# A fused attention and mixer kernel: the order and the queues of its opening loads

## The chip, the cores and the metric

The kernel runs on one core of a Trainium2 chip. The metric is the device time of one execution in microseconds (us); lower is better.

## The reference

Everything starts from one layer norm of x (2048 tokens of 512 values). One branch is attention with 32 heads of 128 against a cached K and V; the other is a mixer with an MLP, whose result gates the attention.

```python
xn = _layernorm(x, axis=-1)
s = _A_ref(xn, A_k_cache, A_v_cache, A_wq, A_wo)     # q = xn @ wq; softmax(q k^T) v; @ wo
g = _silu(_B_ref(xn, B_w1, B_w2, B_w3, B_w4))        # h = gelu(layernorm(xn) @ w1); shifts; @ w2; MLP
return x + s * g
```

## The kernel before

**The whole.** The tokens are cut into 16 tiles of 128. The opening normalises them, transposes them into `xnT` and runs the mixer (`m1`, `m2`) and the first query projections (`q_ahead`). The MLP follows (`m3`, `m4`). Then a long loop over 128 units (8 groups of 4 heads, 4 blocks of 512 tokens) does scores, exponentials, the product with V and the output projection. All but the opening is untouched here.

**What sets the order.** Each engine runs its instructions in the order in which the program writes them: `pin` is the scheduler's `keep_in_program_order`. A DMA is an instruction of the engine that issues it. So what stands behind a waiting DMA issue on ScalarE's queue waits as well, and so on SP's (`nc.sync`).

**The opening loads (L466 to L476).** `load_x` (L159) loads one token tile of 128 KB, `load_w` (L153) the query weights of one head, 128 KB, on SP unless told otherwise. `w1_sb` is the mixer weight, loaded as two halves of 256 KB; `w2_sb` is 512 KB. The line with `junk` (L472) is an activation of one column; ahead of it stands the fetch of the GELU table into ScalarE. In this text x0 is token tile 0, wq0 the query weights of head 0, and so on. The two queues hold before the change:

- ScalarE: x1, x3, the second half of w1, wq0, wq1, wq2, then the table fetch and the small activation
- SP: x0, x2, the first half of w1, x4, x5, x6, x7, wq3, w2, and (L534) x8 to x15

**What uses them.** `ln1(t)` (L489) runs on VectorE: the statistics of tile t+1 (`bn_stats`, L180), then the norm of tile t (L185), with a power on GpSimd in between (L175, L176). `tr_pe(t)` (L195) transposes a tile with four matmuls on TensorE, and ScalarE copies it out of PSUM (L199) into `xnT`. All matmuls go through the helper at L109, so the trace knows them by their tiles: `ps_o<-ident,xall` is a transpose, `ps_m<-xnT,w_sb` the mixer's first product for one tile (`m1_tile`, L495), `ps_q<-xnT,wq_h` a query projection. TensorE's order from L511 on is: transposes of tiles 0 and 1, m1 of tile 0, transposes of tile 2, m1 of tile 1, transposes of tile 3, m1 of tiles 2 and 3; then, four times, a query projection (heads 0 to 3) and the transposes of one of the tiles 4 to 7; then `m2`, which needs w2. Tiles 8 to 15 are transposed by DMA, issued from SP (`tr_dma`, L201), and behind these SP issues the query weights of the last four heads (`wq_e`, L551) and w3. A projection with `wq_e` follows the third block of m1.

Of the kernel before, what the change touches and what calls it, by code (L numbers as in the profile page):

```python
# [17 lines left out]
def kernel(  # L18
# [15 lines left out]
    nc = tc.nc  # L34
# [16 lines left out]
    HG = 4  # L51
# [10 lines left out]
    pin = tc.keep_in_program_order  # L62
# [41 lines left out]
    w1_v = B_w1.rearrange("(dc p) j -> p dc j", p=P)  # L104
# [3 lines left out]
    def mm(out, lhsT, rhs, start, stop):  # L108
# [9 lines left out]
        out=ident[:], in0=diag[:], scalar1=0.0, scalar2=None, op0=ALU.is_equal))  # L118
# [34 lines left out]
    def load_w(h, eng=nc.sync):  # L153
        wqs[h] = wqp.tile([P, DC, Dh], BF16, name="wq_h")
        pin(eng.dma_start(out=wqs[h][:], in_=wq_v[:, :, h * Dh:(h + 1) * Dh]))
# [3 lines left out]
    def load_x(t, eng):  # L159
        xin[t] = tokp.tile([P, D], BF16, tag="ta", bufs=10, name="xin")  # L160
        pin(eng.dma_start(out=xin[t][:], in_=xsrc[t]))
# [3 lines left out]
    w1_sb = pL.tile([P, DC, D], BF16, name="w1_sb")  # L165
# [297 lines left out]

    for t, eng in enumerate([nc.sync, nc.scalar, nc.sync, nc.scalar]):  # L466
        load_x(t, eng)
    pin(nc.sync.dma_start(out=w1_sb[:, 0:2, :], in_=w1_v[:, 0:2, :]))
    pin(nc.scalar.dma_start(out=w1_sb[:, 2:4, :], in_=w1_v[:, 2:4, :]))
    for h in range(HG - 1):  # L470
        load_w(h, nc.scalar)
    pin(nc.scalar.activation(out=junk[:], in_=ones_t[:], func=ACT.Gelu_apprx_tanh))  # L472
    for t in range(4, 8):
        load_x(t, nc.sync)
    load_w(HG - 1)
    pin(nc.sync.dma_start(out=w2_sb[:], in_=w2_v))  # L476
    wps = psX.tile([P, 512], FP32, tag="xm", name="ps_warm")

# [139 lines left out]
    for g in range(NG - 1):  # L618
        b = (g * QT + QT - 1) * HG
        for hh in range(HG):  # L620
            h = (g + 1) * HG + hh
# [234 lines left out]
```

## Time and profile before

| | us |
|---|---|
| median of 3 runs | 1258.79 |
| range of the runs | 1258.17 to 1259.65 |
| the profiled execution | 1256.22 |
| its span, first to last instruction | 1254.4 |

The span is the time from the first to the last instruction of the profiled execution; the rest of its time lies around it. Instructions have their engine, the line of the kernel, the operation, the tile written and the tile read; times run from the span's start. An engine name with q (SPq, ACTq) is its sequencer issuing a DMA. "Busy" is the time an engine worked, and a wait is put down to what came last by the profile.

### The profile page before, as it was taken

Reading aid. Unit: us, or ns where it says so; the run is one execution under the profiler, and the core shown is the slowest. Engines: PE = TensorE matmul, PEld = TensorE weight load, DVE = VectorE, ACT = ScalarE, POOL = GpSimd, SP = SyncE. Lnnn points to the kernel's source line nnn. Section 1 sums busy time; section 2 is a strip of 40 time slices with the busy share of each in tenths; the row PEclk is TensorE's granted clock in tenths of the full one; section 3 lists DMA queues with packets and bytes.
Section 4 is the critical chain, followed back from the end, with each engine's and each line's share of the span. In section 5 each row is a group of like instructions: output and inputs, shape, how many; then the busy total and the mean of one; then the engine's idle time right before and its main releaser. Section 6 shows DMA issues by size and latency. Waiting matters only on the chain.

```text
span 1254.4 us, 16268 instructions
## 1 busy us (share of the span) xinstructions
PE 1237.3 (99%) x5814; PEld 598.7 (48%) x5931; DVE 1031.8 (82%) x1430; ACT 1100.4 (88%) x1117; POOL 35.3 (3%) x91
## 2 busy tenths in 40 slices
PE   8999999999999999999999999999999999999998
PEld 4444444444444444444444444444444444444443
DVE  7721567788988988898888988888888999978888
ACT  4444888999999999999999999999999999998886
POOL 4320000000000000000000000000000000000000
PEclk9999999999999999999999999999999999999999
DMA  6492011435234533544244423453244534442222
GB/s 168 106 163 68 15 28 43 85 85 97 59 78 104 106 52 76 97 102 85 59 90 98 105 48 85 88 118 68 55 102 97 105 68 84 97 93 53 68 56 59
DMA packets 224945, 103.86 MB, mean 83 GB/s; under 512 B 176928, under 2 KB 208160, under 8 KB 224864
## 3 DMA queue, kind: packets, MB, share of 16 engines
q1 hardware_dynamic: 221904, 99.93, 38.0%
q0 software_dynamic: 672, 1.84, 0.9%
q10 hardware_dynamic: 2288, 1.05, 0.3%
q8 instruction: 46, 0.75, 0.3%
q14 instruction: 35, 0.29, 0.1%
HBM read 67.90 MB, written 2.36 MB: 56 GB/s over the span
## 4 chain that ended last, share of the span: by engine, by line
PE 96%; DVE 2%; DMA 1%; issue 1%; ACT 1%; SPq 0%; DVEq 0%; ACTq 0%
PE ps_s L109 39%; PE ps_o L109 36%; PE ps_q L109 9%; PE ps_wo L109 9%; PE ps_m L109 2%; DMA w_sb<-in_B_w_dram 0%; DVE acc L302 0%; DMA rb<-dr 0%; PE ps_sum L109 0%; PE ps_w L109 0%; DMA wq_h<-in_A_wq_dram 0%; ACT qT L277 0%; DVE y L392 0%; DVE xall L420 0%; ACT pT L291 0%
## 5 line engine op out<-in xcount | busy, mean ns | idle before, releaser
L291 ACT ACTIVATE pT<-ps_s 128x1024 bf16<-128x1024 f32 x1024 | 1034.5, 1023 | 76.1 <-PE ps_s L109 28.3
L109 PE MATMUL ps_s<-qT,kT 128*128 128x512 bf16 x2041 | 607.5, 379 | 0.6
L109 PE MATMUL ps_o<-pT,vb 128*128 128x512 bf16 x1962 | 589.0, 379 | 0.5
L302 DVE TENSOR_TENSOR acc<-acc,pT 128x2048 bf16<-128x2048 bf16 x255 | 309.1, 1212 | 77.3 <-ACT pT L291 72.7
L109 PEld LDWEIGHTS <-kT 128*128 128x128 bf16 x2048 | 231.2, 113 | 226.1 <-issue 0.8
L109 PEld LDWEIGHTS <-vb 128*128 128x128 bf16 x2048 | 200.3, 98 | 225.9 <-issue 0.3
L109 PE MATMUL ps_wo<-wo_h,oT 128*128 128x512 bf16 x492 | 177.8, 379 | 2.1
L109 PE MATMUL ps_q<-xnT,wq_h 128*128 128x512 bf16 x481 | 172.9, 379 | 2.1
L297 DVE TENSOR_TENSOR acc<-pT 128x2048 bf16<-128x2048 bf16 x128 | 155.7, 1216 | 6.0 <-ACT pT L291 5.9
L358 DVE TENSOR_TENSOR oT<-ps_o,rb 128x512 bf16<-128x512 f32 x127 | 124.4, 980 | 23.1 <-DMA rb<-dr 22.7
L307 DVE TENSOR_TENSOR acc<-acc 128x1024 bf16<-128x1024 bf16 x127 | 87.8, 692 | 4.3
L275 DVE CAST qT<-ps_q 128x512 bf16<-128x512 f32 x112 | 76.4, 682 | 0.3 <-PE ps_q L109 0.3
L109 PEld LDWEIGHTS <-oT 128*128 128x128 bf16 x508 | 48.5, 98 | 56.2 <-DVE oT L358 0.7
L109 PEld LDWEIGHTS <-wq_h 128*128 128x128 bf16 x484 | 47.2, 98 | 56.1 <-issue 0.2
L411 DVE TENSOR_TENSOR sacc<-ps_wo,sacc 128x512 f32<-128x512 f32 x96 | 66.3, 690 | 3.2 <-PE ps_wo L109 2.7
L338 DVE TENSOR_REDUCE sm<-tT 128x4 f32<-128x512 bf16 x96 | 65.3, 681 | 0.0
L308 DVE TENSOR_TENSOR acc<-acc 128x512 bf16<-128x512 bf16 x127 | 54.0, 425 | 4.3
L242 ACT ACTIVATE h2T<-ps_s 128x1024 bf16<-128x1024 f32 x28 | 28.6, 1023 | 24.1 <-PE ps_s L109 24.1
L109 PE MATMUL ps_s<-xn2T,w_sb 128*128 128x512 bf16 x219 | 48.6, 379 | 0.3
L109 PEld LDWEIGHTS <-w_sb 128*128 128x128 bf16 x336 | 30.4, 98 | 34.5 <-issue 2.3
L109 PEld LDWEIGHTS <-h2T 128*128 128x128 bf16 x224 | 21.5, 98 | 25.0 <-issue 0.2
L109 PE MATMUL ps_m<-w_sb,h2T 128*128 128x512 bf16 x106 | 31.0, 379 | 0.5
(75 smaller groups left out, 333.4 us busy)
## 6 DMA issues: line engine op xcount, KB each, us to landing
rb<-dr SPq DMA_DIRECT2D x127, 256.0 KB, 4.0
vb<-in_A_v_cache_dram SPq DMA_DIRECT2D x64, 256.0 KB, 3.1
wo_h<-in_A_wo_dram SPq DMA_DIRECT2D x32, 128.0 KB, 3.0
wq_h<-in_A_wq_dram SPq DMA_DIRECT2D x29, 128.0 KB, 3.3
w_sb<-in_B_w_dram SPq DMA_DIRECT2D x8, 256.0 KB, 5.7
kT<-in_A_k_cache_dram SPq DMA_TRANSPOSE x128, 3.1
xl<-in_A_x_dram SPq DMA_DIRECT2D x16, 128.0 KB, 3.8
dr<-rc SPq DMA_DIRECT2D x127, 2.0 KB, 1.4
```

Source lines behind the costliest of these rows:

```text
L109: pin(nc.tensor.matmul(out=out, lhsT=lhsT, rhs=rhs, start=start, stop=stop))
L242: pin(nc.scalar.activation(out=h2[c, f][:], in_=ps[:], func=ACT.Gelu_apprx_tanh))
L275: pin(nc.vector.tensor_copy(out=qT[:], in_=st[u].pop("psq")[:]))
L291: pin(nc.scalar.activation(out=s["pT"][-1][:, jj:jj + 2, :], in_=sps[:], func=ACT.Exp, scale=SCALE))
L297: pin(nc.vector.tensor_tensor(out=s["acc"][:], in0=s["pT"][0][:], in1=s["pT"][1][:], op=ALU.add))
L302: pin(nc.vector.tensor_tensor(out=a[:], in0=a[:], in1=st[u]["pT"][i][:], op=ALU.add))
L307: pin(nc.vector.tensor_tensor(out=a[:, 0:2, :], in0=a[:, 0:2, :], in1=a[:, 2:4, :], op=ALU.add))
L308: pin(nc.vector.tensor_tensor(out=a[:, 0, :], in0=a[:, 0, :], in1=a[:, 1, :], op=ALU.add))
L338: pin(nc.vector.tensor_reduce(out=sm[:], in_=s["tT"][:], axis=mybir.AxisListType.X, op=ALU.add))
L358: pin(nc.vector.tensor_tensor(out=to, in0=o, in1=rb, op=ALU.mult))
L411: pin(nc.vector.tensor_tensor(out=sa, in0=ps[:], in1=sa, op=ALU.add))
```

## The change

ScalarE's queue is made to hold x1, the second half of w1, x3, and then the table fetch. All four query weights go to SP's queue, behind x4 to x7 and ahead of w2. Nothing else differs; the loads are the same in number and size.

```diff
-    for t, eng in enumerate([nc.sync, nc.scalar, nc.sync, nc.scalar]):
+    for t, eng in enumerate([nc.sync, nc.scalar, nc.sync]):
         load_x(t, eng)
+    pin(nc.scalar.dma_start(out=w1_sb[:, 2:4, :], in_=w1_v[:, 2:4, :]))
     pin(nc.sync.dma_start(out=w1_sb[:, 0:2, :], in_=w1_v[:, 0:2, :]))
-    pin(nc.scalar.dma_start(out=w1_sb[:, 2:4, :], in_=w1_v[:, 2:4, :]))
-    for h in range(HG - 1):
-        load_w(h, nc.scalar)
+    load_x(3, nc.scalar)
     pin(nc.scalar.activation(out=junk[:], in_=ones_t[:], func=ACT.Gelu_apprx_tanh))
     for t in range(4, 8):
         load_x(t, nc.sync)
-    load_w(HG - 1)
+    for h in range(HG):
+        load_w(h)
     pin(nc.sync.dma_start(out=w2_sb[:], in_=w2_v))
```

## The prediction

> **What bounds the kernel now.** I read the page first, to see which engine the end hangs on.
>
> ```profile
> span 1254.4 us, 16268 instructions
> PE 1237.3 (99%) x5814; PEld 598.7 (48%) x5931; DVE 1031.8 (82%) x1430; ACT 1100.4 (88%) x1117; POOL 35.3 (3%) x91
> ...
> PE 96%; DVE 2%; DMA 1%; issue 1%; ACT 1%; SPq 0%; DVEq 0%; ACTq 0%
> ```
>
> TensorE (PE) is the chain nearly from end to end. So an opening that hands it its work earlier moves the end by as much, unless something with a fixed date holds it again later. The timeline of TensorE over 5 to 14 us shows the opening (start, length, engine, operation, count, and in brackets the idle time before):
>
> ```profile
> 7.07 0.40 PE L109 MATMUL ps_o<-ident,xall 128*128 128x128 bf16 x4 [0.50 <-DVE xall L185]
> 9.78 1.05 PE L109 MATMUL ps_m<-xnT,w_sb 128*128 128x128 bf16 x16 [2.31 <-DMA wq_h<-in_A_wq_dram]
> 10.67 0.39 PE L109 MATMUL ps_o<-ident,xall 128*128 128x128 bf16 x4
> 10.89 1.06 PE L109 MATMUL ps_m<-xnT,w_sb 128*128 128x128 bf16 x16
> 11.79 0.39 PE L109 MATMUL ps_o<-ident,xall 128*128 128x128 bf16 x4
> 12.01 1.95 PE L109 MATMUL ps_m<-xnT,w_sb 128*128 128x128 bf16 x32
> 13.80 0.38 PE L109 MATMUL ps_q<-xnT,wq_h 128*128 128x512 bf16 x1
> ```
>
> After the transposes of tile 1 (7.07) TensorE stands still for 2.31 us before the first mixer matmuls (9.78). These read xnT of tile 0, which ScalarE copies out of PSUM. ScalarE's timeline says why the copy is late:
>
> ```profile
> 1.65 0.46 ACTq L469 DMA_DIRECT2D w_sb<-in_B_w_dram  x1
> 2.13 5.58 ACTq L155 DMA_DIRECT2D wq_h<-in_A_wq_dram  x3
> 7.75 1.28 ACT L472 ACT_TABLE_LOAD   x1 [7.75 <-DMA wq_h<-in_A_wq_dram]
> ...
> 9.15 1.07 ACT L199 ACTIVATE xnT<-ps_o 128x512 bf16<-128x512 f32 x2
> ```
>
> Three wq loads take ScalarE's sequencer 5.58 us, though one issue costs some 0.4; the table fetch (1.28) and the copies of tiles 0 and 1 stand behind them. Narrow windows of the two issuing queues, then the landing column (us from issue to landing) of the DMA view in windows around single issues, explain the 5.58. The landing rows are, in this order, those of x1 and x0, of w1's two halves with x3 and x2, and of x4:
>
> ```profile
> 3.57 0.33 SPq L161 DMA_DIRECT2D xin<-in_A_x_dram  x1
> 4.31 0.80 SPq L161 DMA_DIRECT2D xin<-in_A_x_dram  x2
> 7.34 0.37 ACTq L155 DMA_DIRECT2D wq_h<-in_A_wq_dram  x1
> 7.53 0.38 SPq L155 DMA_DIRECT2D wq_h<-in_A_wq_dram  x1
> ```
> ```profile
> xin<-in_A_x_dram ACTq DMA_DIRECT2D x1, 128.0 KB, 3.0
> xin<-in_A_x_dram SPq DMA_DIRECT2D x1, 128.0 KB, 2.8
> w_sb<-in_B_w_dram SPq DMA_DIRECT2D x1, 256.0 KB, 5.7
> w_sb<-in_B_w_dram ACTq DMA_DIRECT2D x1, 256.0 KB, 5.9
> xin<-in_A_x_dram ACTq DMA_DIRECT2D x1, 128.0 KB, 3.3
> xin<-in_A_x_dram SPq DMA_DIRECT2D x1, 128.0 KB, 3.1
> xin<-in_A_x_dram SPq DMA_DIRECT2D x1, 128.0 KB, 5.8
> ```
>
> x0, issued at 0.73, lands at 3.53, and x5 goes out at 3.57. x2 lands at 4.3, and x6 goes out at 4.31. The halves of w1, issued at 1.65, land at 7.35 and 7.55, and wq2 goes out at 7.34, wq3 at 7.53. Counted over both queues, each new load goes out when the load eight before it has landed. I read this as eight places shared by the two queues; it is inferred from these rows.
>
> **The change part by part.** *ScalarE's queue* then holds x1, half of w1, x3, at some 0.45 us each: free at 2.1 us. The fetch of 1.28 ends at 3.4, and nothing of ScalarE's is due until the transposes of tile 0. These go one tile step before the 7.07 row; a step of VectorE is 1.18 (7.77 to 8.95 below), so they start at 5.9 and end at 6.3. The fetch lies wholly in idle time, with 2.9 us to spare. The copies, two in 1.07 us, follow at 6.4 and 7.5 instead of 9.15.
>
> *TensorE's new start*: tile 0 is in xnT at 7.0, the transposes of tile 1 give TensorE free at 7.4, and w1, unchanged on SP's queue, is in at about 7.35. So the first mixer matmul comes at 7.4 instead of 9.78: 2.38 us gained at this point.
>
> *What is late next* is VectorE. Counting from the mixer's start by the rows above, TensorE wants the transposes of tile 2 after 0.89, at 8.29, and those of tile 3 after 2.01, at 9.41. VectorE's timeline:
>
> ```profile
> 6.92 0.69 DVE L180 BATCH_NORM_STATS2 bn<-xin 128x6 f32<-128x512 bf16 x1
> ...
> 7.77 0.41 DVE L185 TENSOR_SCALAR xall<-xin,mv,rs 128x512 bf16<-128x512 bf16 x1
> ...
> 8.95 0.41 DVE L185 TENSOR_SCALAR xall<-xin,mv,rs 128x512 bf16<-128x512 bf16 x1
> ...
> 13.97 0.69 DVE L180 BATCH_NORM_STATS2 bn<-xin 128x6 f32<-128x512 bf16 x1 [1.08 <-DMA xin<-in_A_x_dram]
> ```
>
> Tiles 2 and 3 are normalised at 8.18 and 9.36, so the cover that TensorE's wait gave VectorE is gone: the slack is 0.1 and then 0.05. Ahead of them stand the statistics of tile 3, at 6.92. *x3 moves behind half of w1 on ScalarE's queue.* Today it lands at 4.5. In its new place it can land as early as that, or as late as x4, which stands behind SP's half of w1 today: 2.12 + 5.8 = 7.9. The nearest row is ScalarE's half of w1: it is today the third load of that queue and lands at 7.55, with the same 512 KB up to its last byte. As w1's half goes out half a us earlier, I take 7.3. The statistics are then 0.38 late, all VectorE work behind them too, and TensorE loses 0.38 less the slack of 0.05: 0.33. Sum so far: 2.38 - 0.33 = 2.05; from the other ends, 2.35 with x3 early and 1.45 with x3 at 7.9.
>
> *The wq loads on SP's queue.* By the count of eight, x6 and x7 go out at x0's and x1's landing (3.6, 3.9), wq0 at x2's (4.3), wq1 to wq3 as w1 and x3 land (7.0 to 8.0), w2 at 8.3 to 8.7. Landing times of today's rows lie between 2.8 and 5.9 us: wq0 is in by 10.2, and TensorE wants it at 13.80 - 2.05 = 11.75. wq1 to wq3 follow on TensorE at about 1.1 us each (four q matmuls at 0.22 to 0.24, by the 32.24 row below, and a tile's transposes at 0.22, from 10.67 to 10.89); issued by 8.2 they land by 14.1, and wq3 is wanted at 15. w2 is wanted four such steps behind the first q matmul, at 16.1, and is in by 14.6. All of this is hidden; without that cover TensorE would lose what is missing, one for one.
>
> *x8 and what hangs on it.* Three wq loads now precede it on SP's queue, and VectorE waits for it, after tile 6, until 13.97.
>
> Rows of the timeline first, then the landings of x8 and of the first wq_e, then the DMA queue's own row for 10 to 14 us (packets, MB, share of the 16 engines):
>
> ```profile
> 8.50 0.50 SPq L161 DMA_DIRECT2D xin<-in_A_x_dram  x1
> 27.41 0.57 SPq L551 DMA_DIRECT2D wq_e<-in_A_wq_dram  x1
> 32.24 3.65 PE L109 MATMUL ps_q<-xnT,wq_e 128*128 128x512 bf16 x15
> ```
> ```profile
> xin<-in_A_x_dram SPq DMA_DIRECT2D x1, 128.0 KB, 5.4
> wq_e<-in_A_wq_dram SPq DMA_DIRECT2D x1, 128.0 KB, 2.4
> q1 hardware_dynamic: 1446, 1.33, 102.8%
> ```
>
> Behind x8 stand the norms of tiles 8 to 15, their DMA transposes and then, in order on SP, the first wq_e, which lands at 29.8. TensorE uses it at 32.24, some 2.35 us later after its weight load: this is the second date that does not move with TensorE, and it caps the gain at 2.35 less any delay of x8. The bytes ahead of x8 are the same in both kernels, and SP's queue alone kept the engines full from 10 to 14 us. So x8 can come 0.5 earlier, because the empty stretch of issues from 5.1 to 7.3 is shorter, or 0.6 later, if its issue slips to 9.1. I take no change, 13.9; at 0.6 late the cap is 1.75. Tile 7, normalised after x8's statistics (13.97 with 0.69 and some 0.5 behind it: 15.2), is wanted by TensorE only at the end of the four steps, near 15.9.
>
> [...]
>
> **The sum**: 2.05, cap not reached, so 2.0 in the span: 1254.4 becomes 1252.4. The profiled execution took 1256.22, 1.8 beyond its span, which the change does not touch; it stands 2.57 below the median of the runs, 1258.79. I carry the difference over: 1256.8.
>
> **The rivals.**
> (a) *x3 arrives in time*, by 6.95. For it: 128 KB loads beside nothing else took 2.8 to 3.3. Against it: x4, the load behind SP's half of w1, landed after that half. Gain 2.35: 1256.4.
> (b) *SP becomes the bound*: three more issues at 0.38 delay x8 by 1.14, to 15.1, and the first wq_e to 30.9; the cap falls to 1.2, the time is 1257.6. Against it: SP stood idle between x7's issue, ended at 5.11, and 7.53, room for all three. For it: if the places are filled, that room is not usable.
> (c) *The change does not do what it says*: the fetch is early, but w1 becomes the wait. x4 to x7 now crowd SP's queue earlier; were w1 in only at 8.4, the gain is 1.4 less VectorE's share, about 1.0: 1257.8.
> (d) *Slower*: SP stops on places. If wq0 to wq3 and w2 each wait for a load before them to land, x8 slips. From 2.35 us late the first wq_e is later than TensorE's old date, and each further us is one lost: 3.0 late gives 1259.4, and 6 late, one more landing time, 1262.4. Against it: after w1's landing the places come free one by one (x8 goes out at 8.50, not a microsecond after wq3), and x4 to x7 hold the next ones.
>
> **How the numbers follow.** Forecast 0.48 (1256.3 to 1257.3 with x3 between 7.1 and 7.6 and the spread of the runs), (a) 0.24, (b) 0.16, (c) 0.05, (d) 0.07. 0.2% is 2.5 us, about what a measurement of this kernel can tell from no change, so "faster" begins below 1256.27. The runs spread over 1.5 us; a fifth of the forecast (0.10) and half of (a) (0.12) fall below it: faster 0.22. Of (d) nearly all of its weight is taken as slower by over 0.2%: 0.06. The rest, 0.72, is within. The range 1255.9 to 1258.4 takes in (a) with the runs' spread, the forecast, (b) and (c); outside lie (d) and tails of 0.1.
>
> **What would show it.** Right: the table fetch at about 2.1 us, the copies of tile 0 and 1 near 6.4 and 7.5, the first mixer matmul near 7.4, VectorE waiting some 0.4 for x3 ahead of tile 3's statistics, the first q matmul near 11.8, TensorE about 2 us ahead at 32 and at 55 us. Wrong: a wait of TensorE at a wq tile or at w2 before 18 us; x8's statistics after 14.6; a wait in front of the first wq_e matmul; a first mixer matmul after 8. If TensorE is 2 us ahead at 55 us and the time is not, something later has taken it, which I do not expect: the view of waits names no wait of TensorE between 20 and 140 us.

## The result, and the profile after

| | before | after |
|---|---|---|
| median of 7 runs (us) | 1258.29 | 1253.59 |
| range of the runs | 1256.56 to 1259.65 | 1253.35 to 1254.06 |
| span of the profiled execution | 1254.4 | 1251.8 |

The ratio is 0.9963, 95% interval 0.9951 to 0.9975: 4.7 us faster, where 2.0 was forecast. The spread fell from 3.1 to 0.7 us. The profiled execution of before took 1256.22, 2.1 under the median of its runs and below all seven; the one of after took 1253.59, its median. So the two profiles differ by 2.6 and the medians by 4.7, and both differences need a cause.

The changed kernel's page and ScalarE's timeline, to be held against the fetch at 7.75 and the copies at 9.15:

```profile
span 1251.8 us, 16270 instructions
```
```profile
2.17 1.28 ACT L471 ACT_TABLE_LOAD   x1 [2.17 <-issue]
3.46 0.20 ACT L471 ACTIVATE junk<-ones_t 128x1 bf16<-128x1 bf16 x1
6.29 0.60 ACT L199 ACTIVATE xnT<-ps_o 128x512 bf16<-128x512 f32 x1 [2.62 <-PE ps_o L109]
7.24 0.60 ACT L199 ACTIVATE xnT<-ps_o 128x512 bf16<-128x512 f32 x1 [0.35 <-PE ps_o L109]
```

ScalarE now waits for TensorE's transposes (2.62 us) and no longer the other way round. TensorE's timeline of the same kernel:

```profile
6.81 0.40 PE L109 MATMUL ps_o<-ident,xall 128*128 128x128 bf16 x4 [0.34 <-DVE xall L185]
7.04 1.06 PE L109 MATMUL ps_m<-xnT,w_sb 128*128 128x128 bf16 x16
7.99 0.40 PE L109 MATMUL ps_o<-ident,xall 128*128 128x128 bf16 x4
8.22 1.06 PE L109 MATMUL ps_m<-xnT,w_sb 128*128 128x128 bf16 x16
9.17 0.40 PE L109 MATMUL ps_o<-ident,xall 128*128 128x128 bf16 x4
9.40 1.95 PE L109 MATMUL ps_m<-xnT,w_sb 128*128 128x128 bf16 x32
11.19 1.03 PE L109 MATMUL ps_q<-xnT,wq_h 128*128 128x512 bf16 x3
```

The mixer starts at 7.04 instead of 9.78, with no wait in front, and the first query projection at 11.19 instead of 13.80: 2.61 earlier. Of the 2.74 gained at the mixer 0.13 are given back, because VectorE now sets the step, as the prediction said of what is late next. Its norms of tiles 2 and 3 are 1.18 apart, where TensorE needed 1.12 for a tile before, and the transposes (7.99, 9.17) begin 0.06 after a norm ends:

```profile
7.52 0.41 DVE L185 TENSOR_SCALAR xall<-xin,mv,rs 128x512 bf16<-128x512 bf16 x1
...
8.70 0.41 DVE L185 TENSOR_SCALAR xall<-xin,mv,rs 128x512 bf16<-128x512 bf16 x1
```

From the first query projection to 50 us the two chains of waits have the same pieces in the same lengths, and the ends of the spans differ by 2.6. The landing column (us from issue), for w1's two halves, x2 and x3, and then for x8:

```profile
w_sb<-in_B_w_dram ACTq DMA_DIRECT2D x1, 256.0 KB, 3.5
w_sb<-in_B_w_dram SPq DMA_DIRECT2D x1, 256.0 KB, 5.0
xin<-in_A_x_dram SPq DMA_DIRECT2D x1, 128.0 KB, 3.0
xin<-in_A_x_dram ACTq DMA_DIRECT2D x1, 128.0 KB, 4.8
```
```profile
xin<-in_A_x_dram SPq DMA_DIRECT2D x1, 128.0 KB, 4.2
```

Issued at 1.17, 1.64, 1.17 and 1.65, they are in at 4.7, 6.6, 4.2 and 6.45. x8, issued at 8.20, is in at 12.4, 1.5 earlier than before.

The earlier opening is the 2.6 of the profiles. The other 2.1 lie between the profile of before and the median of its runs.

### The profile page after: what moved, and what is told of

It is laid out like the page before. It is cut to its first block, busy times and chain, and to the rows that moved or that the text cites. A ratio compares the mean times of both kernels' runs of the same rounds, so it can differ in the third digit from the quotient of the medians.

```text
span 1251.8 us, 16270 instructions
## 1 busy us (share of the span) xinstructions
PE 1237.9 (99%) x5814; PEld 597.8 (48%) x5931; DVE 1031.9 (82%) x1430; ACT 1101.5 (88%) x1117; POOL 35.5 (3%) x91
## 4 chain that ended last, share of the span: by engine, by line
PE 96%; DVE 2%; issue 1%; ACT 1%; DMA 1%; POOL 0%; SPq 0%; DVEq 0%; ACTq 0%
PE ps_s L109 39%; PE ps_o L109 36%; PE ps_q L109 9%; PE ps_wo L109 9%; PE ps_m L109 2%; DVE acc L302 0%; DMA rb<-dr 0%; PE ps_sum L109 0%; PE ps_w L109 0%; DMA xin<-in_A_x_dram 0%; ACT qT L277 0%; DVE y L392 0%; DVE xall L420 0%; ACT pT L291 0%; DVE sacc L411 0%
```

## Experiments

Each kernel ran beside runs of the kernel before on the same chip; a number for before in this section is from those, and it differs a little from chip to chip. The theory that came out of them is **clock**: the gap of TensorE in before costs its own length, and in most runs a spell of half clock behind it. Its rivals were that the runs differ in when w1 lands (**place**, **loads**), in something **later** in the kernel, or in the time around the span (**outside**). "The clock" of a run is the mean that TensorE was granted over its span.

**before_again_a and before_again_b.** The kernel before, unchanged, to see a run at its median.

> The kernel before, unchanged, for a second profile. The profiled execution of before took 1256.22, 2.1 under the median of its runs (1258.29), while the profile of the changed kernel sits at its median. Theory 'place': the runs of before differ because the landing of w1, for which ScalarE's third wq load waits, varies from run to run. Then a run at 1258 shows that issue some 2 us later than 7.34, the first mixer matmul near 11.8 instead of 9.78, and the same lengths behind it. Rival 'later': the opening is the same (mixer at 9.8, first q matmul at 13.8) and the 2 us are lost behind 60 us. Rival 'outside': the span stays 1254.4 and the time around it grows.

> The same once more, for a third profile of the kernel before: theory 'place' expects its time above or below 1256.2 by what its first mixer matmul stands behind or ahead of 9.78; 'later' expects the mixer at 9.8 whatever the time.

Measured: 1258.24 (median of 10; before beside it 1258.20, ratio 0.9999, 0.9989 to 1.0008), profile 1258.3, span 1256.5; and 1257.61, span 1255.8. TensorE in the first:

```profile
10.16 1.13 PE L109 MATMUL ps_m<-xnT,w_sb 128*128 128x128 bf16 x16 [2.83 <-ACT xnT L199]
11.08 0.63 PE L109 MATMUL ps_o<-ident,xall 128*128 128x128 bf16 x4
11.51 1.91 PE L109 MATMUL ps_m<-xnT,w_sb 128*128 128x128 bf16 x16
13.22 0.63 PE L109 MATMUL ps_o<-ident,xall 128*128 128x128 bf16 x4
13.64 2.32 PE L109 MATMUL ps_m<-xnT,w_sb 128*128 128x128 bf16 x32
15.80 1.03 PE L109 MATMUL ps_q<-xnT,wq_h 128*128 128x512 bf16 x3
```

Its busy time in stretches (columns: stretch, length, busy time of TensorE and count, granted clock, DMA share, GB/s), with the same stretch of the first profile of before under it:

```profile
9.50:11.00 1.50, 0.84 (x16) 1.00 0.96 187
11.00:14.40 3.40, 3.40 (x36) 0.50 1.03 351
14.40:17.00 2.60, 2.55 (x35) 1.00 0.29 93
```
```profile
11.00:14.40 3.40, 3.35 (x55) 1.00 0.92 305
```

The second repeat has its low stretch earlier:

```profile
9.60:13.00 3.40, 3.30 (x32) 0.50 0.97 314
```

The mixer is only 0.38 later than 9.78, because w1 lands 0.4 later. But from 11.00 to 14.40 the clock is granted at 0.50, and 16 mixer matmuls, 1.06 long in the first profile, take 1.91. From the mixer's start to the first projection it is 5.64 us instead of 4.02: 1.6 for the clock. The second repeat has the mixer at 9.70 and the projection at 15.27, that is 5.57, with the half clock from 9.6 to 13.0. Theory 'place' is wrong as it stood: the landing explains 0.4 and not 2. 'Later' and 'outside' are wrong: from the first projection to the span's end it is 1240.6, 1240.7 and 1240.5 us in the three profiles.

**two_wq.** Before, with wq2 on SP's queue:

```diff
-    for h in range(HG - 1):
+    for h in range(HG - 2):
         load_w(h, nc.scalar)
...
+    load_w(HG - 2)
     load_w(HG - 1)
```

> The kernel before with one load moved: wq2 from ScalarE's queue to SP's, so that ScalarE has x1, x3, half of w1, wq0, wq1 and the table fetch. Only the load that waits for w1 is gone from its queue. Theory 'place': ScalarE is free at 4.1, the fetch ends at 5.4 in idle time, the first mixer matmul comes at 7.0 to 7.5 and the time is that of the changed kernel, 1253.6 within 0.6. Rival 'bytes' (what helps is that w1 has no wq loads beside it on the other queue): w1 lands as late as before, after 7.3, the mixer starts at 7.5 or later and at least a quarter of the gain is missing: 1254.5 to 1256.

Measured: 1254.12, ratio to before 0.9967 (0.9954 to 0.9980). The fetch is at 3.98, the copies at 6.17 and 7.29. One load, the one that waited for w1, carried nearly the whole cost; two wq loads on ScalarE did no harm to the copies. What its profile has and that of the changed kernel has not is a short wait of TensorE for w1, in its timeline:

```profile
7.09 0.28 PE L109 MATMUL ps_m<-xnT,w_sb 128*128 128x128 bf16 x2
7.66 0.95 PE L109 MATMUL ps_m<-xnT,w_sb 128*128 128x128 bf16 x14 [0.29 <-DMA w_sb<-in_B_w_dram]
```

Rival 'bytes' asked for 1254.5 or more, so the time does not bear it out. Nor can the wait of 0.29 be put down to the wq loads beside w1: the next kernel has none there and waits as well.

**wq_sp.** All wq loads on SP, but x3 ahead of w1's half on ScalarE's queue, as before had it:

```diff
-    for h in range(HG - 1):
-        load_w(h, nc.scalar)
     pin(nc.scalar.activation(out=junk[:], in_=ones_t[:], func=ACT.Gelu_apprx_tanh))
     for t in range(4, 8):
         load_x(t, nc.sync)
-    load_w(HG - 1)
+    for h in range(HG):
+        load_w(h)
```

> The kernel before with all wq loads on SP's queue and the table fetch behind x1, x3 and half of w1, in before's order: x3 ahead of the half of w1, unlike the changed kernel. The prediction took x3's new place for a cost of 0.33; the profile of the changed kernel shows x3 landing at 6.45, ahead of its use at 6.66. Theory 'no cost': 1253.6 within 0.4. Rival 'x3 costs': 0.3 better, 1253.2. Rival 'w1 earlier': the changed order gets w1's half in at 4.7 and that helps; here the half lands near 6.5 and the mixer starts later than 7.04 by up to 0.4, 1254.

Measured: 1253.63, ratio 0.9962 (0.9949 to 0.9975). The mixer waits 0.23 for w1 (start 7.57) in its profile, and the median is that of the changed kernel. The landing of w1's two halves:

```profile
w_sb<-in_B_w_dram SPq DMA_DIRECT2D x1, 256.0 KB, 5.9
w_sb<-in_B_w_dram ACTq DMA_DIRECT2D x1, 256.0 KB, 6.1
```

Issued at 1.64 and 1.65, they are in at about 7.5 and 7.7, as late as in before, though no wq load stands on ScalarE's queue. With x3 behind ScalarE's half they are in at 4.7 and 6.6 (changed kernel), so the earlier w1 goes with that order and not with the wq loads. Neither it nor x3's place shows in the time; whether the two cancel can't be told.

**before_warm4, before_warm6 and before_warm9.** Before, with matmuls on zeros in TensorE's gap; the loads and their order stay:

```diff
     ln1(1, tr_pe)
+    warm_mm(4)     # 6 and 9 in the other two
     pm = [m1_tile(0, psX, "xa")]
```

> The same with four extra matmuls on zeros, 0.86 us, which leave a gap of some 1.5 to 2 us. Theory 'clock': the fall of the clock becomes rarer or goes; the median lies at 1256 to 1257.5, between before and the kernel with nine. If a gap of 1.5 us is harmless, 1256.2. Rival 'loads': 1258.2.

> The kernel before with six extra matmuls on zeros behind the transposes of tile 1 (1.3 us; they compute nothing). With nine, the profile shows the clock whole and the opening 1.4 us shorter than in before's own profiles at half a clock, but also a wait of 1.0 us for a K load at 1130 us, which with four is not there. Theory 'clock': with six the clock is whole in nearly all runs and the median is that of four or better, 1255.5 to 1256.2. Rival 'fill costs' (the extra matmuls bring a loss of their own that grows with their number): between four and nine, 1256.3 to 1256.8.

> The kernel before with nine extra matmuls on a tile of zeros behind the transposes of tile 1 (they add work and compute nothing of the reference's); at 0.215 us each they fill 1.9 of the 2.3 to 2.8 us in which TensorE waits for ScalarE. No load and no wait is moved. Two more profiles of the kernel before show the granted TensorE clock at 0.50 for some 3.4 us behind that gap, the first one at 1.00 all through. Theory 'clock': with the gap filled the clock stays at 1.00, the mixer still starts at 9.7 to 10.2, and the time is that of before's runs with a full clock: 1255.9 to 1256.5, where before has a median of 1258.2. Rival 'loads': the runs of before differ through the landings; the filling changes nothing, 1258.2 within 0.5.

Measured: four 1255.93 (0.9988, 0.9979 to 0.9998), nine 1256.96 (0.9994, 0.9985 to 1.0004), both beside before at 1257.67; six 1257.65 (0.9992, 0.9982 to 1.0001) beside before at 1258.39. With four, the mean clock is 0.999 or 1.000 in eight of ten runs (1254.96 to 1256.93) and 0.997 or 0.998 in the two slowest (1258.19, 1258.60). With six and nine it is never below 0.999, but their intervals take in 1: no gain is shown for them. The profile with four is the opening of before's first profile, at a full clock and 0.17 earlier:

```profile
9.61 1.05 PE L109 MATMUL ps_m<-xnT,w_sb 128*128 128x128 bf16 x16 [1.49 <-DMA wq_h<-in_A_wq_dram]
...
13.63 1.03 PE L109 MATMUL ps_q<-xnT,wq_h 128*128 128x512 bf16 x4
```

Filling part of the gap kept the clock in eight of ten runs, and with four it gives back 1.7 us; the two runs of before with a clock of 0.999 beside it took 1255.32 and 1255.62. Six and nine did not give the time that the theory wanted: with six, five runs have a clock of 1.000, and three of them took 1257.99 to 1258.61, the other two 1255.58 and 1256.51. So a full clock alone does not give the short time. Their profiles lose nothing in the opening but have waits in the long loop, in the view of waits the first rows (nine above, six below):

```profile
PE ps_s L109 <- DMA kT<-in_A_k_cache_dram: 1.0, 1, 1.0
```
```profile
PE ps_sum L109 <- DVE qT L275: 1.8, 1, 1.8
PE ps_w L109 <- DVE oT L358: 0.6, 1, 0.6
```

The order of SP's loads is the same with nine as with four. Whether these late waits belong to the shifted start or come by chance was not settled; they are not in the profiles of before or of the changed kernel, which have no wait of TensorE above 0.4 us behind 20 us.

**fetch_first.** Before, with the fetch ahead of the wq loads, which stay on ScalarE's queue:

```diff
-    for h in range(HG - 1):
-        load_w(h, nc.scalar)
     pin(nc.scalar.activation(out=junk[:], in_=ones_t[:], func=ACT.Gelu_apprx_tanh))
+    for h in range(HG - 1):
+        load_w(h, nc.scalar)
```

> The kernel before with only the table fetch and its small activation moved ahead of the three wq loads; these stay on ScalarE's queue. Theory 'place': ScalarE is still held by wq2's issue until w1 has landed, 7.0 to 7.5, then copies tiles 0 and 1 at 7.5 to 7.9; the mixer starts at 8.1 to 8.5, half way. The gap of TensorE is 0.8 to 1.2 us, too short for the clock to fall. Time 1253.6 + 1.1 to 1.4 = 1254.7 to 1255.0. Rival 'fetch' (the fetch itself was the whole cost, the issues nothing): mixer at 7.1, 1253.6. If the clock falls all the same, 1256 to 1257.

Measured: 1254.93, ratio 0.9981 (0.9972 to 0.9991), beside before at 1257.67. ScalarE's timeline, then a row of TensorE's:

```profile
2.14 1.28 ACT L470 ACT_TABLE_LOAD   x1 [2.14 <-issue]
3.22 0.39 ACTq L155 DMA_DIRECT2D wq_h<-in_A_wq_dram  x1
...
4.37 3.40 ACTq L155 DMA_DIRECT2D wq_h<-in_A_wq_dram  x2
7.81 1.08 ACT L199 ACTIVATE xnT<-ps_o 128x512 bf16<-128x512 f32 x2 [4.17 <-DMA w_sb<-in_B_w_dram]
```
```profile
8.46 1.05 PE L109 MATMUL ps_m<-xnT,w_sb 128*128 128x128 bf16 x16 [1.49 <-ACT xnT L199]
```

The copies still wait for w1's landing, through wq2's issue; the fetch in front of them was worth its 1.28 and the issue the rest. As forecast, the mixer comes half way. The gap is 1.49 us, where 0.8 to 1.2 was expected. That such a gap is too short for the clock to fall was the author's estimate; the nearest row was the first profile of before, with 2.31 us and a full clock. The clock was 0.997 or 0.998 in three of ten runs (1256.70 to 1257.02), which was expected only as an exception. How long the gap was in these three is not on record, and it moves with w1's landing: wq2's issue ended anywhere from 6.8 to 8.3 in the profiles of before and of its three filled versions. That 1.5 us is enough is not shown.

**after_no_warm.** The changed kernel without its twelve warm-up matmuls:

```diff
-    warm_mm(11)
+    warm_mm(1)
...
-    warm_mm(1)
     ln1(1, tr_pe)
```

The upper place keeps one matmul, so eleven of the twelve are gone.

> The changed kernel without the warm-up matmuls on zeros at its start (eleven and one). They compute nothing; TensorE then first works at 5.7. Theory 'clock': the clock is at half for some 3.4 us from the transposes of tile 0 or 1 on, through the mixer's tiles; each of their groups takes about twice as long, and the time is 1.5 to 3 us above 1253.6: 1255 to 1256.6. Rival 'loads': the clock is nothing to this opening, which waits for copies and loads; 1253.6 within 0.4.

Measured: 1255.09, ratio 0.9979 (0.9970 to 0.9989): 1.0 to 1.5 over the changed kernel (1253.59 and, below, 1254.09). TensorE and its stretch:

```profile
7.12 1.91 PE L109 MATMUL ps_m<-xnT,w_sb 128*128 128x128 bf16 x16
8.82 0.63 PE L109 MATMUL ps_o<-ident,xall 128*128 128x128 bf16 x4
9.25 1.20 PE L109 MATMUL ps_m<-xnT,w_sb 128*128 128x128 bf16 x16
```
```profile
8.00:9.00 1.00, 1.00 (x12) 1.00 1.05 232
```

16 matmuls take 1.91 as in before's half clock, although the clock column reads 1.00: twelve matmuls in this microsecond, where the changed kernel has twenty. What half speed does to this opening is thus seen a second time, with no gap ahead of the mixer and in the changed order of the loads. That it is the clock is inferred here, from the 1.91 alone.

**after_held and after_again.** The changed kernel with ScalarE held back by activations on zeros, and the changed kernel once more:

```diff
     pin(nc.scalar.activation(out=junk[:], in_=ones_t[:], func=ACT.Gelu_apprx_tanh))
+    for _ in range(11):
+        pin(nc.scalar.activation(out=held[:], in_=warm[:], func=ACT.Identity))
```

> The changed kernel, with all its loads where it has them, but ScalarE held back: eleven extra activations on a tile of zeros (128x512, some 0.5 us each, of no use to the reference) behind the small activation keep it busy to about 9.2 us. The mixer then starts near 9.8, as in before, behind a gap of TensorE of some 2.5 us; every landing is that of the changed kernel. Theory 'clock' (a gap of this length costs its own length and then half a clock for some 3.4 us): 1253.6 + 2.7 + 1.6 = 1257.9 in most runs, mean clock 0.996 to 0.998, the tiles of the mixer at half speed in most profiles. Rival 'gap only': 1256.3, clock 0.999 to 1.000. Rival 'loads' (part of before's time is in the order of its loads and not in ScalarE's lateness): below 1256.

> The changed kernel once more, on the chip of these runs, for a second profile and its own spread: 1253.6 within 0.4, clock 0.999 to 1.000; first mixer matmul 7.0 to 7.3, x3's landing ahead of 6.7, no wait of TensorE longer than 0.5 us between 7 and 20 us.

Measured: after_again 1254.09, ratio to before (1258.39) 0.9970 (0.9958 to 0.9981), mixer at 7.43 in its profile because x0 landed at 3.6 instead of 3.3. Both are just outside what was expected. Held, 1260.18, ratio 1.0015 (1.0005 to 1.0024). The activations took 0.66 us each and not 0.5, so the gap became 3.70 and not 2.5. TensorE, and one short stretch of it:

```profile
11.33 1.87 PE L110 MATMUL ps_m<-xnT,w_sb 128*128 128x128 bf16 x16 [3.70 <-ACT xnT L200]
12.99 0.63 PE L110 MATMUL ps_o<-ident,xall 128*128 128x128 bf16 x4
13.42 1.32 PE L110 MATMUL ps_m<-xnT,w_sb 128*128 128x128 bf16 x16
...
16.59 0.59 PE L110 MATMUL ps_q<-xnT,wq_h 128*128 128x512 bf16 x2
```
```profile
10.70:10.80 0.10, 0.00 (x0) 0.50 1.10 328
```

All ten runs have a clock of 0.996 to 0.998. With the gap as it came out, the theory's sum is 1254.09 + 3.9 (mixer at 11.33 instead of 7.43) + 1.6 = 1259.6; 1260.18 was measured. In this profile the half clock begins inside the gap, so less of it falls on work: from the mixer to the first projection it is 5.26 us instead of 4.15 (after_again), 1.1 for the clock and not 1.6. The profile has a wait of 0.8 us for VectorE in the loop besides. 'Gap only' would give 1258.0 and 'loads' less. With every load in its new place, lateness of ScalarE alone costs the gap and the clock. That the time is even above that of before fits the mixer's start, 1.2 to 1.6 us later than in the three profiles of before.

The 21 runs of before beside these two divide by the clock without overlap: four at 1.000 take 1255.74 to 1256.30, and seventeen at 0.996 to 0.998 take 1257.14 to 1259.97. Their medians are 1255.96 and 1258.76.

The clock of a run takes some care. It also counts the end of the kernel, where TensorE has no matmul left and the clock is low again, here in before_again_a:

```profile
1254.00:1256.50 2.50, 0.00 (x0) 0.50 0.16 52
```

The mean of 0.997 in that profile is 3.2 us of clock lost in 1256.5: 1.7 in the opening and 1.5 at this idle end. In the changed kernel's profile, with 0.999, the clock is below 1.00 only at that end, from 1248.4 on. A mean of 0.996 is, as an estimate, a loss of 4.4 us or more (0.0035 of 1257), and seven of the seventeen have it, with a median of 1259.41. No run with 0.996 was profiled. So why the medians lie 2.8 apart, where the profiles show 1.6, stays open; a longer spell in these runs is one possibility.

## Why the prediction was wrong, point by point

**The step that failed** is the last one of the sum: "it stands 2.57 below the median of the runs, 1258.79. I carry the difference over". It was carried as a constant, with no reason given why the change should leave it alone. The runs show a spell of half clock in its place, which cost 1.6 us in each of two further profiles and which the one profiled execution happened not to have and most later runs of before have. The change closes the gap that it stood behind: every run of the changed kernel has a clock of 0.999 or 1.000, and with the gap put back (after_held) all ten have 0.996 to 0.998. For before's runs in the first comparison the clock is not on record, so there the spell is inferred. On the chip of the last pair: from before's median, 1258.39, to its four runs of full clock, 1255.96, is 2.4 us; from there to the changed kernel, 1254.09, is 1.9. The forecast of 2.0 is of the second part only. In the first comparison the parts are 2.1 and 2.6, so it is near that part, and in one of its terms by luck: the 0.33 taken off for x3 did not occur.

The gap itself is in the prediction, as an idle time of 2.31 us of TensorE. The prediction does not speak of the clock, which was 1.00 there; that was a fact of that execution and not of the kernel. In the two repeats, with gaps of 2.83 and 2.51 us, it was granted at 0.50 for 3.4 us each (11.00 to 14.40, 9.6 to 13.0). In the first it fell 0.84 us after the mixer's start at 10.16, in the second 0.1 ahead of it (9.70). What sets that moment, and which gap is long enough, no run shows.

**Point by point.** *ScalarE's queue*: right. Fetch at 2.17 (2.1 forecast), copies at 6.29 and 7.24 (6.4, 7.5). *The start of the mixer*: 7.04 against 7.4, in a second profile 7.43; x0's landing (3.3 and 3.6) sets it. *w1*: 6.6 against 7.35; two_wq and wq_sp, with x3 ahead of ScalarE's half as in before, have its last half in at about 7.7 and wait 0.29 and 0.23 for it, so the earlier landing goes with x3's new place. *x3's cost of 0.33*: mis-sized. It landed at 6.45, ahead of its use at 6.66, and cost nothing; wq_sp, with x3 in its old place, takes the same time. This is rival (a), which gave 2.35. *wq loads and w2*: hidden, as worked out; no wait of TensorE at either. *x8 and the first wq_e*: x8 came 1.5 earlier instead of not at all, so VectorE's wait for it is gone and the first wq_e goes out at 26.06 instead of 27.41; the cap was not reached, as no wait stands in front of its use at 29.63. *The count of eight*: the dates go by it in the changed kernel too. wq0 goes out at 4.23 as x2 lands (4.2), wq1 at 4.70 as ScalarE's half of w1 does (4.7), wq2 at 6.69 as SP's does (6.6). That these are eight places shared by the two queues is the author's reading of the dates. *Rivals (b), (c), (d)*: SP was no bound, w1 no new wait in the two profiles of the changed kernel, and nothing was slower. *Three more issues on SP*, the price in rival (b): it did not show, since the landings just named, and not the issues at 0.37 to 0.51 each, go with SP's dates.

## What to carry to other kernels

When the profiled execution is faster than the runs by more than their spread allows, its profile lacks something that the runs have; ask for a second one before carrying the difference as a constant. Here, with TensorE the chain for 96% of the span, closing its gap of 2.31 us brought the mixer 2.74 earlier and the span's end 2.6, and in two profiles 1.6 us more were lost behind gaps of 2.5 and 2.8; so a change that closes a gap can be worth more than the gap. Three DMA issues held ScalarE for 5.58 us, the last until w1 had landed at 7.35, with the table fetch queued behind them: look up when the loads ahead land before putting a load on an engine that has other work.

## What the runs showed of the hardware

Of three profiles of before, the one with a gap of 2.31 us kept the full clock, and those with 2.51 and 2.83 had a spell of 3.4 us at half the clock; so had the one profile of after_held, with 3.70 (10.6 to 14.0). In the clocks of the runs, seventeen of 21 runs of before had such a loss, three of ten of fetch_first, two of ten of before_warm4 and ten of ten of after_held; the gaps of these runs were not measured. In one profile the spell began after work had resumed (11.00, with the mixer at 10.16). Its cost was 1.6 us in two profiles and 1.1 in the third; between the medians of the two kinds of runs lie 2.8. And the granted clock in the profile read 1.00 in after_no_warm (8.00 to 9.00) while 16 matmuls took 1.91 us, where the changed kernel has 1.06: there the length of a known matmul group tells more than the column.
